# Decay attention and routed experts on one core: causal scores packed two heads to 192 columns, products of the attention done in halves of 64 rows of output

## The chip, the core and the metric

One NeuronCore of a Trainium2 chip runs the whole program in one launch. The metric is the device time of that launch in microseconds (us). TensorE (PE) does the matrix products and loads a stationary operand before each of them (the profile lists these loads as PEld), VectorE (DVE) and ScalarE (ACT) work on elements, GpSimd (POOL) and SyncE (SP) here mostly issue DMAs.

## The reference

Linear attention with a complex decay per token and feature runs over 768 tokens for 4 batches and 8 heads of 48 features; its output goes through a mixture of 8 experts, to which tokens are assigned greedily with a capacity.

```python
scale = np.minimum(mag, 0.999) / (mag + 1e-06)          # mag = |a|
for t in range(S):
    new_re = ar * S_re - ai * S_im
    new_im = ar * S_im + ai * S_re
    kv = np.einsum('bhd,bhe->bhde', k[:, :, t], v[:, :, t])
    S_re, S_im = (new_re + kv, new_im)
    y[:, :, t] = np.einsum('bhd,bhde->bhe', q[:, :, t], S_re)
...
logits = x @ w_gate                                     # x: y, all heads of a token
...
h = np.maximum(x[mask] @ w1[e], 0.0)
out[mask] = h @ w2[e]
```

## The kernel before

The program has two parts, `attention` and `experts`. Attention goes through 24 units of 128 tokens, six units to a batch (`cc` is the number of a unit in its batch, 0 to 5). ACT and DVE first turn the decays of three units at a time into running magnitudes and angles and rotate and scale k and q with them; a unit's k and q of all heads (96 real numbers each, cosine and sine part) then go by eight DMAs through the tile `f` into the tile `KQ` (96 x 8 heads x 257: 128 columns of k, 128 of q, one of decay). After that a unit consists of these steps, whose names in the code stand in brackets:

- scores (`SC`, twice, four heads each): `sc` = k-transposed times q, 128 keys by 128 queries for each head;
- mask (`MK`, twice, on DVE): `am` = `sc` times the causal mask, so keys after the query count nothing;
- flip (`FL`, twice, units with `cc` under 5): `kp` = k with tokens in rows, by PE transposes; ACT copies it to `kt` (`KC`);
- state (`ST`): `U` = `kt`-transposed times v, for each head 96 x 48, with tokens as the contraction; `carry` (`CA`, `cc` over 0) adds the old state `W` by a product with the identity, 96 x 384; DVE multiplies by the decay into the next `W` (`WM`);
- mix (`MX`): `y` = v-transposed times `am`, plus (`cc` over 0) `W`-transposed times q. Each head's output has 64 rows (48 and 16 of the next head), so two heads lie in the lower and the upper half of `y`, and their products stand next to each other;
- turn back (`XC`, `FN`, `XE`): ACT copies `y` to `xT`, PE turns it with the matrix `pick` (tokens in rows, and the router's logits beside them) into `xp`, ACT copies that to `x`, and it is stored.

Each of these products is fp32: one instruction of the program becomes two passes on PE, each with its own load of weights (192 score products are x384 in the profile); a transpose is one pass. The order of all instructions on every engine is fixed beforehand: `in_order` plays the steps through with a cost for each and a priority from the table `OFF`, and a helper class records them (so nearly all have its line, L137). Where its play leaves PE idle, products into the tile `hot` are put in, which nobody reads.

`attention` is followed by the routing of tokens and the experts, for which PE multiplies in three fp32r products.

Of the kernel before, what the change touches and what calls it, by code (L numbers as in the profile page):

```python
# [8 lines left out]
F32 = mybir.dt.float32  # L9
# [47 lines left out]
def constants(nc, con, z, w_gate):  # L57
    v, g = nc.vector, nc.gpsimd

    def t(n, shape, dt=F32):  # L60
        x = con.tile(shape, dt, name=n)
        setattr(z, n, x)
        return x
# [3 lines left out]
    v.tensor_scalar(t("ident", [128, 128]), jp, 0.0, None, op0=OP.is_equal)  # L67
    v.tensor_scalar(t("mask", [128, 128]), jp, 0.0, None, op0=OP.is_ge)
    t("tri", [128, 128], BF)
# [33 lines left out]


GROUPS = [(b, c, GC) for b in range(B) for c in range(0, S // 128, GC)]
CUTS = {0: [(0, 1), (1, GC)], 7: [(0, 2), (2, GC)]}
# [135 lines left out]
def attention(nc, real, tc, z, q, k, a_re, a_im, v_tok, xd, later):  # L242
# [9 lines left out]
    for i in range(2):  # L252
        w = con.tile([96, 400], F32, name=f"W{i}")
        g.memset(w, 0.0)
        W.append(w)
    for i in range(2):
        x = con.tile([128, GC, 432], F32, name=f"V{i}")
        g.memset(x[:, :, 384:], 0.0)
        VT.append(x)
# [205 lines left out]
    def unit(i):  # L465
# [8 lines left out]
        def KQ():  # L474
            return tiles["KQ", i]

        for hh in range(2):
            def scores(hh=hh):
                sc = ps.tile([128, 4, 128], F32, name="sc", bufs=2)
                mine["sc", hh] = sc  # L480
                for h in range(4):
                    nc.tensor.matmul(sc[:, h], KQ()[:, hh * 4 + h, :128], KQ()[:, hh * 4 + h, 128:256], start=True, stop=True)

            def mask(hh=hh):
                a = wk.tile([128, 4, 128], F32, name="am", bufs=4)
                v.tensor_tensor(a, mine["sc", hh], z.mask[:, None].to_broadcast([128, 4, 128]), op=OP.mult)
                mine["am", hh] = a
            op(("SC", i, hh), "pe", 0.9, at - 0.5, scores, KD + [("MK", i - 1, hh)])
            op(("MK", i, hh), "dve", 0.64, at, mask, [("SC", i, hh), ("MX", i - 2)])
        if cc < 5:  # L490
            for hh in range(2):
                def flip(hh=hh):
                    kp = ps.tile([128, 4, 96], F32, name="kp", bufs=2)
                    mine["kp", hh] = kp
                    for h in range(4):
                        nc.tensor.transpose(kp[:, h], KQ()[:, hh * 4 + h, :128], z.ident[:96, :96])

                def copy(hh=hh):
                    if "kt" not in mine:
                        mine["kt"] = wk.tile([128, 8, 96], F32, name="kt")  # L500
                    nc.scalar.activation(mine["kt"][:, hh * 4:hh * 4 + 4], mine["kp", hh], AF.Copy)
                op(("FL", i, hh), "pe", 0.34, at - 0.45, flip, KD + [("KC", i - 1, hh), ("KC", i - 2, hh)])
                op(("KC", i, hh), "act", 0.44, at, copy, [("FL", i, hh), ("ST", i - 2), ("ST", i - 3)])

            def state():
                U = ps.tile([96, 384], F32, name="U")
                mine["U"] = U
# [22 lines left out]
        def mix():  # L530
            Wc = W[cc % 2]
            y = ps.tile([128, 4, 128], F32, name="y")
            mine["y"] = y
            for p in range(4):
                for inter in range(2 if cc else 1):
                    for h in (2 * p, 2 * p + 1):
                        o = y[64 * (h % 2):64 * (h % 2) + 64, p]
                        e = slice(h * 48, h * 48 + 64)
                        if inter:
                            nc.tensor.matmul(o, Wc[:, e], KQ()[:, h, 128:256], start=False, stop=True)  # L540
                        else:
                            nc.tensor.matmul(o, v_[:, c, e], mine["am", h // 4][:, h % 4], start=True, stop=(cc == 0))

# [635 lines left out]
def experts(nc, tc, z, router, w1, w2, xd, out):  # L1179
# [152 lines left out]
    for n in range(WARM):  # L1332
        o = plan.tensor.matmul(hot[:, n % 3], z.mask, z.ident, start=True, stop=True)
        o.kind, o.main = "warm", True
        o.deps.append(router.placed)
# [59 lines left out]
def _lay_out(inputs):  # L1395
    import numpy as np

    def feature_major(a):
        a = a.reshape(B, H, S, 3, 16).transpose(0, 3, 4, 1, 2)
        return np.ascontiguousarray(a).reshape(B, 3, 128, S)  # L1400

    c = np.ascontiguousarray
    return {
# [3 lines left out]
        "a_im": feature_major(inputs["a_im"]),  # L1407
        "v": c(inputs["v"].transpose(0, 2, 1, 3)).reshape(N, DM),
        "w_gate": c(inputs["moe_w_gate"]).reshape(4, 2, D, E),
# [18 lines left out]
```

## Time and profile before

| | us |
|---|---|
| median of 3 runs (527.74 to 534.6) | 533.71 |
| the profiled execution's own time | 531.14 |
| its span, first to last instruction | 529.4 |
| first scores to the last turn back, in the span | 39.9 to 241 |
| routing of the first expert, then experts | 241 to 529 |

The page gives busy time by engine, but matmuls are pipelined, so the busy time of PE is more than what its products need one after the other. What a product needs is read from the starts in the timeline: the start of one kind of product to the start of the next, over the number of passes. The chain of work that ended last says where PE, DVE or a DMA held up the end.

### The profile page before, as it was taken

What the parts mean: (1) busy time and instruction counts of PE and PEld (TensorE: products, weight loads), DVE (VectorE), ACT (ScalarE), POOL (GpSimd) and SP (SyncE); (2) the same over time, 40 slices, a digit from 0 to 9 for tenths busy, and PEclk for the clock granted to TensorE, in tenths of its full rate; (3) what the DMA queues carried; (4) which work ended last, traced back from release to release, by engine and by line L of the source; (5) the groups of instructions that cost most, each with busy time, mean ns of one, the idle gap of its engine ahead of it and who ended that gap; (6) DMA issues with size and microseconds to landing.
All of it is one profiled execution on the core that took longest, in us unless ns stands there. A gap on an engine that the chain in (4) does not pass through costs nothing.

```text
span 529.4 us, 9655 instructions
## 1 busy us (share of the span) xinstructions
PE 451.3 (85%) x3626; PEld 395.3 (75%) x3635; DVE 410.5 (78%) x1192; ACT 271.6 (51%) x418; POOL 81.2 (15%) x95
## 2 busy tenths in 40 slices
PE   0009889898979999996699799999999999999993
PEld 0007769596868788995588468888888888999993
DVE  6989878999979999834847499889898987974330
ACT  6996848796949695611011513343252544363421
POOL 3000000000000000000021320522322242450202
PEclk9999989999989999997589999999999999999997
DMA  8866878897978776731260703544161521950101
GB/s 256 252 176 154 236 201 252 210 244 232 253 204 256 206 240 171 194 81 46 80 206 1 298 30 120 175 169 150 46 251 62 230 84 42 402 195 4 46 0 45
DMA packets 48909, 86.03 MB, mean 163 GB/s; under 512 B 5344, under 2 KB 43744, under 8 KB 46816
## 3 DMA queue, kind: packets, MB, share of 16 engines
q1 hardware_dynamic: 39104, 42.56, 28.1%
q0 software_dynamic: 6304, 38.16, 21.1%
q10 hardware_dynamic: 3456, 4.72, 2.5%
q8 instruction: 28, 0.46, 0.4%
q14 instruction: 17, 0.14, 0.1%
HBM read 53.49 MB, written 9.44 MB: 119 GB/s over the span
## 4 chain that ended last, share of the span: by engine, by line
PE 42%; DVE 18%; DMA 17%; issue 10%; ACT 5%; SPq 4%; POOL 2%; POOLq 0%; DVEq 0%; ACTq 0%
PE acc L137 24%; PE y L137 4%; SPq L137 4%; DMA xg<-xd,idx 4%; PE sc L137 4%; PE U L137 4%; DMA s<-s 3%; ACT s L137 3%; DMA ar<-in_a_re 3%; PE cnt L137 2%; DMA V<-in_v 2%; DVE f L137 2%; DVE hl L137 2%; DMA KQ<-f 2%; DVE neg L137 2%
## 5 line engine op out<-in xcount | busy, mean ns | idle before, releaser
L137 PE MATMUL sc<-KQ 96*128 96x128 f32 x384 | 50.2, 284 | 41.0 <-DMA KQ<-f 40.9
L137 PEld LDWEIGHTS sc<-KQ 96*128 96x128 f32 x384 | 47.4, 198 | 44.3 <-DMA KQ<-f 41.8
L137 ACT ACTIVATE hh<-acc 128x384 fp32r<-128x384 f32 x56 | 27.0, 491 | 77.4 <-PE acc L137 77.2
L137 PE MATMUL acc<-xh,w1l 128*128 128x384 f32 x168 | 55.8, 345 | 0.0
L137 PE MATMUL acc<-xh,w1h 128*128 128x384 f32 x168 | 55.7, 345 | 0.0
L137 PE MATMUL acc<-xl,w1h 128*128 128x384 f32 x168 | 54.9, 340 | 0.0
L137 PE MATMUL acc<-w2h,hl 128*128 128x384 f32 x168 | 54.0, 348 | 0.0
L137 PE MATMUL acc<-w2l,hh 128*128 128x384 f32 x168 | 53.5, 346 | 0.5 <-DVE w2l L137 0.5
L137 PE MATMUL acc<-w2h,hh 128*128 128x384 f32 x168 | 53.9, 345 | 0.0
L137 DVE TENSOR_TENSOR ind<-m,thr 128x768 bf16<-128x768 f32 (+1 forms) x45 | 34.0, 774 | 15.3 <-PE thr L137 14.7
L137 DVE TENSOR_TENSOR f<-kq,CS 128x768 f32<-128x768 f32 x48 | 43.5, 951 | 0.2 <-ACT CS L137 0.2
L137 POOL DMA_INDIRECT out<-ot,idx x24 | 26.3, 1095 | 96.3 <-ACT ot L137 92.4
L137 DVE SCALAR_TENSOR_TENSOR hl<-acc,hh 128x384 fp32r<-128x384 f32 x56 | 30.3, 552 | 13.4 <-ACT hh L137 12.8
L137 PE MATMUL y<-am,V 128*64 128x128 f32 x384 | 38.3, 289 | 1.4 <-ACT xT L137 0.9
L137 ACT ACTIVATE ot<-acc 128x384 f32<-128x384 f32 x24 | 11.8, 491 | 54.0 <-PE acc L137 35.3
L137 DVE TENSOR_TENSOR am<-sc,mask 128x512 f32<-128x512 f32 x48 | 32.1, 682 | 4.3 <-PE sc L137 4.1
L137 POOL DMA_INDIRECT xg<-xd,idx x24 | 27.6, 1149 | 48.1 <-issue 22.3
L137 PE MATMUL xp<-pick,xT 112*128 112x104 f32 x192 | 26.8, 283 | 6.9 <-ACT xT L137 4.7
L137 PEld LDWEIGHTS acc<-w2l,hh 128*128 128x128 f32 x168 | 31.0, 188 | 1.6 <-DVE w2l L137 1.0
L137 PEld LDWEIGHTS acc<-xh,w1h 128*128 128x128 f32 x168 | 31.2, 188 | 1.2 <-DVE ic L137 0.4
L137 PE MATMUL y<-KQ,W 96*64 96x128 f32 x320 | 31.9, 277 | 0.2 <-DVE W L137 0.2
L137 PEld LDWEIGHTS xp<-pick,xT 112*128 112x128 f32 x192 | 24.0, 194 | 10.7 <-ACT xT L137 6.8
(184 smaller groups left out, 1074.7 us busy)
## 6 DMA issues: line engine op xcount, KB each, us to landing
KQ<-f SPq DMA_DIRECT2D x192, 96.4 KB, 2.5
kq<-in_k SPq DMA_DIRECT2D x8, 576.0 KB, 5.2
kq<-in_q SPq DMA_DIRECT2D x8, 576.0 KB, 7.0
V<-in_v SPq DMA_DIRECT2D x8, 576.0 KB, 9.2
xd<-x ACTq DMA_DIRECT2D x24, 192.0 KB, 2.8
ar<-in_a_re SPq DMA_DIRECT2D x6, 576.0 KB, 4.7
ai<-in_a_im SPq DMA_DIRECT2D x6, 576.0 KB, 6.9
s<-s POOLq DMA_DIRECT2D x6, 576.0 KB, 7.9
```

The costliest lines, as they stand in the source:

```text
L137: r = f(*a, **k)
```

## The change

Four things change; the steps, their costs in the planner and their priorities stay.

Scores leave out the keys 64 to 127 for the queries 0 to 63 (never causal). For a pair of heads, `he` and `ho`, `sc` holds 192 columns in place of 256. The first 64 hold the keys 0 to 63 and queries 0 to 63 of both heads, `he` in the top half and `ho` in the low half; the next 64 the queries 64 to 127 of `he` with all its keys; the last 64 the same of `ho`, with its two halves of keys exchanged. That is four products a pair, each with 64 columns of weights, instead of two with 128. The mask gets the same form, and `am` has 384 columns, not 512.

Because odd heads now have their keys exchanged, so have v (exchanged on the host, in the layout of the input) and k with tokens in rows: the flip is no transpose any more but, for each head, two fp32 products with the identity, one for each half of the tokens. Its copy goes to one of two fixed tiles `KT` with 32 columns of zeros behind.

The state (`U`, now 128 rows) and the turn back (`xp`) are done in two products each, for the low 64 and the high 64 columns of the weights, into the two halves of the output.

The mix first does the queries 0 to 63 of all eight heads, with 64 keys each; then, by pairs of heads, the queries 64 to 127 with 128 keys and, where there is an old state, the product with `W` as before.

```diff
         for hh in range(2):
             def scores(hh=hh):
-                sc = ps.tile([128, 4, 128], F32, name="sc", bufs=2)
+                sc = ps.tile([128, 512], F32, name="sc", bufs=2)[:, :384].rearrange("p (a b) -> p a b", a=2)
                 mine["sc", hh] = sc
-                for h in range(4):
-                    nc.tensor.matmul(sc[:, h], KQ()[:, hh * 4 + h, :128], KQ()[:, hh * 4 + h, 128:256], start=True, stop=True)
+                for p in range(2):
+                    he, ho = hh * 4 + 2 * p, hh * 4 + 2 * p + 1
+                    packed = sc[:, p].rearrange("p (a b) -> p a b", a=3)
+                    for r, h, keys, o, queries in ((0, he, 0, packed[:, 0:2], 0), (1, ho, 0, packed[:, 0::2], 0),
+                                                   (0, ho, 1, packed[:, 2], 1), (1, he, 1, packed[:, 1], 1)):
+                        nc.tensor.matmul(o[HALVES[r]], KQ()[:, h, HALVES[keys]], KQ()[:, h, 128 + 64 * queries:256],
+                                         start=True, stop=True)
...
-                a = wk.tile([128, 4, 128], F32, name="am", bufs=4)
-                v.tensor_tensor(a, mine["sc", hh], z.mask[:, None].to_broadcast([128, 4, 128]), op=OP.mult)
+                a = wk.tile([128, 2, 192], F32, name="am", bufs=4)
+                v.tensor_tensor(a, mine["sc", hh], z.mask[:, None].to_broadcast([128, 2, 192]), op=OP.mult)
...
                     for h in range(4):
-                        nc.tensor.transpose(kp[:, h], KQ()[:, hh * 4 + h, :128], z.ident[:96, :96])
+                        for r in range(2):
+                            nc.tensor.matmul(kp[HALVES[r], h], KQ()[:, hh * 4 + h, HALVES[(r + h) % 2]], z.ident[:96, :96],
+                                             start=True, stop=True)
...
                 for h in range(8):
-                    nc.tensor.matmul(U[:, h * 48:h * 48 + 48], mine["kt"][:, h], v_[:, c, h * 48:h * 48 + 48],
-                                     start=(h == 0), stop=(h == 7 and not cc), skip_group_check=True)
+                    for r in HALVES:
+                        nc.tensor.matmul(U[r, h * 48:h * 48 + 48], KT[i % 2][:, h * 96 + r.start:h * 96 + r.stop],
+                                         v_[:, c, h * 48:h * 48 + 48], start=(h == 0), stop=(h == 7 and not cc), skip_group_check=True)
...
+            heads = [(h, y[HALVES[h % 2], h // 2], slice(h * 48, h * 48 + 64), mine["am", h // 4][:, h // 2 % 2]) for h in range(8)]
+            for h, o, e, a in heads:
+                r = HALVES[h % 2]
+                nc.tensor.matmul(o[:, :64], v_[r, c, e], a[r, :64], start=(h < 2), stop=(cc == 0), skip_group_check=True)
             for p in range(4):
...
+                for h, o, e, a in heads[2 * p:2 * p + 2]:
+                    b_ = 64 + 64 * (h % 2)
+                    nc.tensor.matmul(o[:, 64:], v_[:, c, e], a[:, b_:b_ + 64], start=False, stop=(cc == 0), skip_group_check=True)
+                if cc:
+                    for h, o, e, a in heads[2 * p:2 * p + 2]:
+                        nc.tensor.matmul(o, Wc[:, e], KQ()[:, h, 128:256], start=False, stop=True, skip_group_check=True)
...
             for p in range(4):
-                nc.tensor.matmul(xp[:, p, :104], mine["xT"][:112, p], z.pick[:112, p], start=True, stop=True)
+                for r in HALVES:
+                    nc.tensor.matmul(xp[r, p, :104], mine["xT"][:112, p, r], z.pick[:112, p], start=True, stop=True)
```

On PE, in the steps of one unit with an old state (tile names with the numbers of V, W and KT; the size is that of the output), the order before is:

```order
L137 MATMUL kp<-ident,KQ 128x96 x8
L137 MATMUL U<-W_111,ident 96x384
L137 MATMUL sc<-KQ 128x128 x8
L137 MATMUL U<-V_113,kt 96x48 x8
L137 MATMUL xp<-pick,xT 128x104 x4
L137 MATMUL y<-am,V_113 64x128 x2
L137 MATMUL y<-KQ,W_109 64x128 x2
```

and at the same place in the changed program:

```order
L142 MATMUL kp<-ident,KQ 64x96 x16
L142 MATMUL U<-W_115,ident 96x384
L142 MATMUL sc<-KQ 64x128
L142 MATMUL sc<-KQ 64x2x64
L142 MATMUL sc<-KQ 64x64 x2
...
L142 MATMUL U<-V_121,KT_117 64x48 x16
L142 MATMUL xp<-pick,xT 64x104 x8
L142 MATMUL y<-am,V_121 64x64 x10
L142 MATMUL y<-KQ,W_113 64x128 x2
```

No step changes its place: every step stands where it stood, with twice as many products in it (the three rows of `sc` come four times). On ACT and SP the order is the same row for row. On DVE the masks' sizes change, and at the start of the program four small operations build the mask matrix in place of one. The place on DVE where the masks of a unit stand between the router's work on the first 18 units' logits and the element work, before:

```order
L137 TENSOR_REDUCE qm<-q_2045 128x18
L137 TENSOR_TENSOR oh<-q_2045,qm 128x144
L137 TENSOR_TENSOR am<-sc,mask 128x512 x2
L137 COPY tl<-neg 128x3
L137 TENSOR_SCALAR zi<-s_1535 128x3x128
L137 TENSOR_SCALAR neg<-neg 128x3x256
```

and in the changed program:

```order
L142 TENSOR_REDUCE qm<-q_2649 128x18
L142 TENSOR_TENSOR oh<-q_2649,qm 128x144
L142 TENSOR_TENSOR am<-sc,mask 128x384 x2
L142 COPY tl<-neg 128x3
L142 TENSOR_SCALAR zi<-s_1968 128x3x128
L142 TENSOR_SCALAR neg<-neg 128x3x256
```

Only the size of the two masks is another, 384 columns for 512.

## Rows read from the trace of the kernel before

**Rows 1.** The page, busy us by engine (share of span) and instructions.

```profile
PE 451.3 (85%) x3626; PEld 395.3 (75%) x3635; DVE 410.5 (78%) x1192; ACT 271.6 (51%) x418; POOL 81.2 (15%) x95
```

**Rows 2.** Busy time by stretch: PE, PEld, DVE, ACT, POOL; clock, DMA share, GB/s.

```profile
60.00:100.00 40.00, 35.33 (x318) 27.85 (x321) 34.84 (x61) 30.59 (x37) 1.26 (x2) 0.96 0.82 227
100.00:140.00 40.00, 36.70 (x374) 31.78 (x376) 37.31 (x67) 31.68 (x38) 1.69 (x2) 1.00 0.84 226
180.00:205.00 25.00, 23.89 (x259) 21.96 (x257) 24.79 (x52) 16.19 (x24) 0.00 (x0) 1.00 0.78 225
205.00:241.00 36.00, 35.85 (x400) 32.81 (x401) 22.51 (x45) 17.79 (x31) 0.00 (x0) 1.00 0.49 127
```

**Rows 3.** Chain that ended last: start, us, what (x passes or instructions).

```profile
43.35 2.50 PE sc L137 x10
...
74.97 2.62 PE U L137 x18
...
182.41 1.20 DVE am L137 x2
...
204.48 0.61 DVE am L137
205.13 1.25 PE y L137 x16
...
239.91 1.08 PE xp L137 x8
```

**Rows 4.** Timeline of PE, 213 to 222 us: start, us, operation, shapes, passes.

```profile
213.11 0.88 PE L137 MATMUL kp<-ident,KQ 96*128 96x96 f32 x8
213.83 0.81 PE L137 MATMUL U<-W,ident 96*96 96x384 f32 x2
214.47 1.95 PE L137 MATMUL sc<-KQ 96*128 96x128 f32 x16
216.26 1.48 PE L137 MATMUL U<-V,kt 128*96 128x48 f32 x16
217.58 1.10 PE L137 MATMUL xp<-pick,xT 112*128 112x104 f32 x8
218.61 0.44 PE L137 MATMUL y<-am,V 128*64 128x128 f32 x4
...
219.10 0.39 PE L137 MATMUL y<-am,V 128*64 128x128 f32 x4
219.32 0.39 PE L137 MATMUL y<-KQ,W 96*64 96x128 f32 x4
...
220.52 0.89 PE L137 MATMUL U<-W,ident 96*96 96x384 f32 x2
221.25 0.82 PE L137 MATMUL kp<-ident,KQ 96*128 96x96 f32 x8
```

**Rows 5.** Timeline of the weight loads, 218.60 to 218.70 us.

```profile
218.61 0.20 PEld L137 LDWEIGHTS y<-am,V 128*64 128x64 f32 x4
```

**Rows 6.** Operations on the tile `am`, 198 to 241 us: ns min/median/max.

```profile
L137 PEld LDWEIGHTS y<-am,V x96: 132/136/138, 205.1 to 239.3; 128*64 128x64 f32 x96
```

**Rows 7.** Groups by form, 0 to 250 us: busy, mean ns, idle before.

```profile
L137 DVE TENSOR_TENSOR am<-sc,mask 128x512 f32<-128x512 f32 x48 | 32.1, 682 | 4.3 <-PE sc L137 4.1
L137 PE MATMUL hot<-cold 128*128 128x512 bf16 x63 | 16.3, 395 | 0.4 <-issue 0.2
L137 DVE TENSOR_TENSOR W<-U,KQ 96x384 f32<-96x384 f32 x20 | 11.0, 548 | 8.3 <-PE U L137 5.6 <-DMA KQ<-f 2.7
```

**Rows 8.** Timeline, 208 to 209 us: copy of the flip, and the state.

```profile
208.04 0.87 ACT L137 ACTIVATE kt<-kp 128x384 f32<-128x384 f32 x2
...
208.85 0.38 PE L137 MATMUL U<-V,kt 128*96 128x48 f32 x3
```

**Rows 9.** Timeline, 247 us: a count of the routing.

```profile
247.10 1.04 PE L137 MATMUL cnt<-oh,ind 128*32 128x8 bf16 x24 [2.02 <-DVE ind L137]
```

**Rows 10.** The page, DMA queues: packets, MB, share of 16 engines' span.

```profile
q8 instruction: 28, 0.46, 0.4%
```

More of the change, by code (lines that the diff above doesn't have):

```diff
@@ L67, in constants @@
     v.tensor_scalar(t("ident", [128, 128]), jp, 0.0, None, op0=OP.is_equal)
-    v.tensor_scalar(t("mask", [128, 128]), jp, 0.0, None, op0=OP.is_ge)
+    mask = t("mask", [128, 192])
+    top, low = HALVES
+    for r, o, i in ((slice(0, 128), slice(64, 128), low), (top, top, top), (low, top, low), (top, slice(128, 192), top)):
+        v.tensor_scalar(mask[r, o], jp[r, i], 0.0, None, op0=OP.is_ge)
+    g.memset(mask[low, 128:192], 1.0)
     t("tri", [128, 128], BF)
@@ L102, in best @@
     v.tensor_tensor(oh, q, bc(qm, E), op=OP.is_equal)
+HALVES = (slice(0, 64), slice(64, 128))
 GROUPS = [(b, c, GC) for b in range(B) for c in range(0, S // 128, GC)]
@@ L255, in attention @@
         W.append(w)
+    KT = []
+    for i in range(2):
+        x = con.tile([128, 800], F32, name=f"KT{i}")
+        g.memset(x[:, 768:], 0.0)
+        KT.append(x)
     for i in range(2):
@@ L495, in flip @@
                     for h in range(4):
-                        nc.tensor.transpose(kp[:, h], KQ()[:, hh * 4 + h, :128], z.ident[:96, :96])
+                        for r in range(2):
+                            nc.tensor.matmul(kp[HALVES[r], h], KQ()[:, hh * 4 + h, HALVES[(r + h) % 2]], z.ident[:96, :96],
+                                             start=True, stop=True)
                 def copy(hh=hh):
-                    if "kt" not in mine:
-                        mine["kt"] = wk.tile([128, 8, 96], F32, name="kt")
-                    nc.scalar.activation(mine["kt"][:, hh * 4:hh * 4 + 4], mine["kp", hh], AF.Copy)
+                    nc.scalar.activation(KT[i % 2][:, hh * 384:hh * 384 + 384].rearrange("p (a b) -> p a b", a=4), mine["kp", hh], AF.Copy)
                 op(("FL", i, hh), "pe", 0.34, at - 0.45, flip, KD + [("KC", i - 1, hh), ("KC", i - 2, hh)])
@@ L505, in state @@
             def state():
[L506 to L507 removed]
+                U = ps.tile([128, 384], F32, name="U")
+                mine["U"] = U[:96]
                 for h in range(8):
[L509 to L510 removed]
+                    for r in HALVES:
+                        nc.tensor.matmul(U[r, h * 48:h * 48 + 48], KT[i % 2][:, h * 96 + r.start:h * 96 + r.stop],
+                                         v_[:, c, h * 48:h * 48 + 48], start=(h == 0), stop=(h == 7 and not cc), skip_group_check=True)
             def carry():
@@ L1332, in experts @@
     for n in range(WARM):
-        o = plan.tensor.matmul(hot[:, n % 3], z.mask, z.ident, start=True, stop=True)
+        o = plan.tensor.matmul(hot[:, n % 3], z.mask[:, :128], z.ident, start=True, stop=True)
         o.kind, o.main = "warm", True
@@ L1400, in feature_major, with swapped @@
         return np.ascontiguousarray(a).reshape(B, 3, 128, S)
+    def swapped(a):
+        a = np.ascontiguousarray(a).reshape(B, S // 128, 2, 64, H // 2, 2, D)
+        a[..., 1, :] = a[:, :, ::-1, ..., 1, :].copy()
+        return a.reshape(N, DM)
     c = np.ascontiguousarray
```

10 lines of the change are left out of this document (1 added, 9 removed).

## Prediction

> **What bounds the kernel now.** Read the table by stretch first. Attention is the span to 241 us, and no engine bounds all of it: from 60 to 140 us PE and DVE are each busy about nine tenths of the time and the DMA engines over eight tenths; from 180 to 205 us DVE is busy for 24.79 of 25 us; from 205 to 241 us PE has no gap and DVE little to do [rows 2]. Then the chain of work that ended last: PE holds it in stretches that begin at 43 and 75 us and, the longest, at 205 us, running on to the last turn back at 241; in between, masks and other work of DVE do (182 to 205 us) [rows 3], or DMAs. The whole of attention is in series with the experts, whose instructions don't change. So an edit on PE counts where the chain is on PE, and an edit on DVE where DVE is.
>
> I counted the chain's PE pieces from 43 to 241 us (the first and last stand in [rows 3]): scores of 9.9 units, flips of 7, states of 9, turns back of 9, mixes of 11 (two of them without an old state), and 8 carries. Of masks there are 9.
>
> **Price of a pass.** A fp32 pass goes by its columns: the carry's two passes of 384 take 0.64 us (213.83 to 214.47), 0.00083 a column; 16 score passes of 128 take 1.79, 0.112 each, so a fixed part of about 0.005 [rows 4]. The state has 48 columns in a pass but takes 1.32/16 = 0.0825 (216.26 to 217.58) [rows 4]: its load of 96 columns sets that, 0.00086 a column, 0.055 for 64. In the mix, two heads in two halves of the output run side by side: a group of four passes takes 0.22 (219.10 to 219.32) [rows 4], 0.11 a pair, what one score pass takes alone.
>
> Do loads run side by side too? Four mix loads take 0.20 together [rows 5], and one lasts 0.136 [rows 6]. So all four begin within 0.064, where one after the other at 0.055 would need 0.165: they go in twos. A pair of passes with 64 columns each should then take 0.053 + 0.005 = **0.058**, with 96 columns 0.085, with 104 0.092. No row shows a pair that short; the bounds are 0.055 (the loads) and 0.11 (the mix's pair). I take 0.058, since rows 4 to 6 give it from both sides, columns and loads.
>
> **The change, part by part** (us for one unit on PE).
> - Scores: 1.79 before; a head pair is now two pair-passes of 128 and two of 64, so 8 x 0.112 + 8 x 0.058 = 1.36: -0.43.
> - Flip: 8 transposes, one pass each. They take 0.72 behind a mix [rows 4], 0.68 at 0.085 a pass. Now 32 passes in 16 pairs, 1.36: +0.68. This is the one part that plainly gets dearer.
> - State: 1.32 to 16 x 0.058 = 0.93: -0.39.
> - Turn back: 8 x 0.112 = 0.90 (128 columns of weights) to 8 x 0.092 = 0.74: -0.16.
> - Mix: 16 x 0.11 = 1.76 to 8 x 0.11 for the old state and 16 x 0.058 for `am`: 1.81, +0.05. No column is saved here; the same 128 are cut in two.
> - Switches between whole and half width. Into the mix: turn back to mix takes 1.03 for 0.90 of work; inside it, 1.91 for 1.76; the carry behind it 0.73 (220.52 to 221.25), 0.64 otherwise [rows 4]. That is 0.37 for in and out. Before, the mix alone is in halves. Now all is, but the carry is not, and the first part of the mix has 64 rows of keys instead of 128. With a carry, that is four switches a unit for two, if the change of rows costs what the change of columns does: +0.37. No row shows a change of rows; bounds 0 and +0.37. I take the upper one, the nearest row.
>
> The Trainium skill speaks against the change here: "TensorEngine Tiling (Array Packing)", section "Key Properties", says that changing the tiling mode drains TensorE, a change of tile does not. The trace agrees for columns (0.73 against 0.64, [rows 4]); by the rule the rows count too, and the term is +0.37, otherwise 0.
>
> So a unit with an old state (16 of 24 have state and carry) gains 0.93 and pays 1.10. On the chain: 9.9 x -0.43 + 7 x 0.68 + 9 x -0.39 + 9 x -0.16 + 11 x 0.05 + 8 x 0.37 = -4.26 + 4.76 - 3.51 - 1.44 + 0.55 + 2.96 = -0.9. One gain on it is lost: the state at 208.85 starts as the copy of the flip on ACT ends (208.04 + 0.87) [rows 8], so scores that end sooner before it win nothing: +0.4.
>
> - Masks: 384 columns for 512. The decay product has that form from PSUM, 548 ns for 682 [rows 7]: 48 x 0.134 = 6.4 us of DVE. On the chain 9, so -1.2. The bound is every mask before 205 us, 38 x 0.134 = -5.1, if DVE's queue passes all of it on.
> - At the start: three more small operations on DVE and three fills on POOL while DVE and POOL wait for the first loads; ACT's copies keep their sizes; the DMAs, and the queues of SP and ACT, are untouched; the host exchanges v without device time. Nothing.
>
> Sum: -0.9 + 0.4 - 1.2 = **-1.7**, so 531.14 gives 529.4. The profiled execution is 0.5% under the median of 533.71, from which it gives 532.0. I forecast **531**, the middle: no change that a measurement tells apart, since that needs about 2%, 10.7 us.
>
> **Rivals.**
> 1. *PE cannot take passes that fast* (slower). A unit has 162 passes with a load instead of 82, and every gain above rests on pairs at 0.058, 0.029 a pass. Before, PE takes 84 passes in 8.14 us (213.11 to 221.25), 0.097 each, and its fastest long run is the mix, 0.055 to 0.06 [rows 4]; only 24 passes of the routing go at 0.043 [rows 9]. If 0.055 a pass is what PE can be fed, every pair takes 0.11: 40 pairs of 64 at +0.054, 16 of 96 at +0.027, 8 of 104 at +0.02, +2.7 a unit, x 9 on the chain = +24, less the 1.7: 554. It also needs some 3,500 more instructions on top of 7,261 [rows 1], 14 more packets on the 28 of about 1.2 us (0.4% of 16 x 529 us) [rows 10], the same kind of limit. It decides from about 0.078 a pair, where 9 x 64 pairs x 0.02 are 11 us. Against it: loads that start within 0.064 in fours, and the 0.043. The fill products, 16.3 us [rows 7], leave PE some room off the chain.
>
> The skill's "TensorE: Matmul & The Clock Gate", section "Back-to-back issue gap", has a floor of about 25 ns for small matmuls, and 62 ns where the sequencer decodes them; by the latter a unit is 162 x 0.062 = 10.0, an estimate, and by the former nothing changes. No row here decides between them.
>
> 2. *More gain than the chain shows* (faster, but hardly by 2%). Rows cost no switch (-3.0) and all masks pass on (-3.9 more): -8.6, 522.5. For it: DVE's 24.79 of 25 us. Against: the DMA share over 0.8 where the chain leaves both engines.
>
> 3. *The masks become the wait.* The mix now begins with all eight heads, so both masks must be there 0.23 us after its start (8 passes at 0.029), not 0.9 (16 at 0.055). At 204.48 the first of two masks is on the chain and the mix starts at 205.13 [rows 3], 0.6 before the second can end; PE then stands about 0.4, with XC, FN and the flips queued behind it and ACT's copy of `y` waiting. At every one of 11 mixes: +4.4, 534 to 536; within 2%.
>
> **How the numbers follow.** Forecast case (527 to 534) 0.62; rival 2 0.15, of which I put a third over 2%, since the runs of before alone scatter by 1.3%; rival 3 0.06; rival 1 0.17. That the halves don't run side by side at all is excluded by rows 4 to 6. So faster 0.05, same 0.78, slower 0.17. The range takes in rival 2 to its price and the smaller prices of a pair of rival 1 (0.08 to 0.09), up to 545; outside are 0.05 below and 0.14 above.
>
> **What would show it.** In the changed trace, start to start: scores 1.36, flip 1.36, state 0.93, turn back 0.74 plus 0.1 to 0.2 at a switch, first part of the mix 0.46, `am` masks 548 ns; the stretch from the 20th unit's flip to the last turn back within 1 us of before. Pairs at 0.08 or more, or idle PE with cause "issue" inside a run of passes, show rival 1; PE idle inside a mix for DVE's mask, rival 3. What would make me wrong most is the 0.058, which no row of before has.

## The result and the profile after

The changed kernel is slightly slower: 535.49 us median of 20 executions (531.66 to 538.64) beside 534.15 (527.26 to 541.63) for the kernel before, ratio 1.0087, interval 1.0059 to 1.0114. Within 2% it is no change, as forecast, but forecast was a gain of 0.5%, and the interval leaves that out. The ratio leaves out executions more than 1.5% above the fastest of their kernel, which are 7 of the 20 of the kernel before and none of the changed one; over all executions the medians differ by 0.25% only, and the means by 1.5 us with an uncertainty of 2.0. So a gain is not there, and the size of the loss is less sure than the interval alone says. The profiled execution took 533.22 us (span 531.4) beside 531.14 (529.4).

The page after, busy time by engine and the queue of instruction packets:

```profile
PE 451.1 (85%) x5386; PEld 389.7 (73%) x5395; DVE 405.0 (76%) x1195; ACT 273.1 (51%) x418; POOL 81.4 (15%) x98
...
q8 instruction: 42, 0.69, 0.5%
```

PE does 1,760 passes more in the same busy time, and DVE is busy 5.5 us less [rows 1]; there are 14 more instruction packets, as forecast. The busy time by stretch, columns as in [rows 2]:

```profile
60.00:100.00 40.00, 34.95 (x607) 27.71 (x606) 33.88 (x61) 31.18 (x38) 1.68 (x2) 0.96 0.81 226
100.00:140.00 40.00, 37.18 (x708) 31.50 (x708) 32.75 (x60) 28.64 (x36) 0.84 (x1) 0.91 0.80 219
180.00:205.00 25.00, 23.91 (x480) 20.04 (x481) 23.66 (x50) 18.01 (x27) 0.00 (x0) 1.00 0.73 209
```

DVE is no longer full from 180 to 205 us, and the clock from 100 to 140 us is 0.91 on the mean, where it was 1.00. The last turn back starts at 243.74 us, before at 241.79; from the router's first product on, at 245.48 us and before at 243.73, 285.9 us of the span are left, before 285.7. So the 2.0 us that the two profiled executions differ by arise in attention, and not in its last stretch, which PE fills: from the flip at 208.39 us to the turn back at 242.04 are 33.65 us, and before, from 206.32 to 239.84, 33.52.

They arise between the sixth and the seventh turn back. PE's timeline there, first before, then after:

```profile
95.88 1.14 PE L137 MATMUL xp<-pick,xT 112*128 112x104 f32 x8 [0.73 <-ACT xT L137]
...
105.44 0.30 PE L137 MATMUL kp<-ident,KQ 96*128 96x96 f32 x1 [0.94 <-DMA KQ<-f]
...
112.94 1.03 PE L137 MATMUL xp<-pick,xT 112*128 112x104 f32 x8
```
```profile
96.22 0.93 PE L142 MATMUL xp<-pick,xT 112*64 112x104 f32 x16 [1.28 <-ACT xT L142]
...
106.76 0.59 PE L142 MATMUL kp<-ident,KQ 96*64 96x96 f32 x4 [2.24 <-DMA KQ<-f]
...
110.52 2.77 PE L142 MATMUL sc<-KQ 96*64 96x128 f32 x32
113.08 1.18 PE L142 MATMUL U<-V,KT 128*64 128x48 f32 x32
...
117.10 0.93 PE L142 MATMUL xp<-pick,xT 112*64 112x104 f32 x16
```

The distance to before grows from 0.34 to 4.16 us, and half of it is made up later. The flip waits 2.24 us for the stacked keys (0.94 before), and behind this gap the granted clock is 0.50, the lower of its two levels (1.2 GHz of 2.4), and the scores take 2.56 us (110.52 to 113.08), for 1.39 at the full clock below. The busy time of two stretches:

```profile
104.00:106.00 2.00, 0.52 (x14) 0.33 (x9) 0.96 (x2) 1.16 (x1) 0.00 (x0) 1.00 0.24 75
...
108.00:110.00 2.00, 2.00 (x34) 1.88 (x32) 1.86 (x2) 0.50 (x1) 0.00 (x0) 0.50 1.08 369
```

That is one execution of each kernel. In the profiles of two runs below that are as slow, e14 and e17, the clock from 100 to 140 us is 1.00, so this drop isn't the cause in all.

The timeline of PE, the same place as [rows 4]: start, us, operation, shapes, passes.

```profile
215.48 1.49 PE L142 MATMUL kp<-ident,KQ 96*64 96x96 f32 x32
216.90 0.89 PE L142 MATMUL U<-W,ident 96*96 96x384 f32 x2
217.72 1.56 PE L142 MATMUL sc<-KQ 96*64 96x128 f32 x32
219.11 1.09 PE L142 MATMUL U<-V,KT 128*64 128x48 f32 x32
220.03 0.90 PE L142 MATMUL xp<-pick,xT 112*64 112x104 f32 x16
220.86 0.95 PE L142 MATMUL y<-am,V 64*64 64x64 f32 x20
...
222.97 0.89 PE L142 MATMUL U<-W,ident 96*96 96x384 f32 x2
223.78 1.54 PE L142 MATMUL kp<-ident,KQ 96*64 96x96 f32 x32
```

From start to start: flip 1.42 (215.48 to 216.90), of which 0.1 is the change to the carry, and 1.37 behind a carry (223.78 to 225.15); scores 1.39, state 0.92, turn back 0.83, mix 2.11, carry 0.81. One unit with state and carry: 215.48 to 223.78 less one carry of 0.81 is 7.49 us; before, 213.11 to 221.25 less 0.64 is 7.50 [rows 4]. On PE alone the change is even. The weight loads of the mix's first part, and the groups by form:

```profile
213.47 0.31 PEld L142 LDWEIGHTS y<-am,V 64*64 64x64 f32 x8
```
```profile
L142 DVE TENSOR_TENSOR am<-sc,mask 128x384 f32<-128x384 f32 x48 | 25.7, 549 | 7.2 <-PE sc L142 6.5
...
L142 DVE TENSOR_TENSOR W<-U,KQ 96x384 f32<-96x384 f32 x20 | 11.0, 548 | 11.2 <-PE U L142 11.2
```

Eight loads in 0.31 us: by twos as the four of [rows 5]. The masks take 549 ns, and 6.4 us of DVE are gone. But read the idle time behind the second bar: it was 5.6 us for `W` behind PE and 4.1 for `am` [rows 7]. The waits in attention, 40 to 245 us (total us, times, longest):

```profile
DVE W L142 <- PE U L142: 11.2, 7, 3.5
...
PEld kp L142 <- DMA KQ<-f: 8.4, 13, 2.4
...
DVE am L142 <- PE sc L142: 6.5, 9, 2.2
DVE f L142 <- DMA KQ<-f: 5.3, 6, 2.3
...
PE y L142 <- DVE am L142: 0.3, 1, 0.3
```

These DVE waits were 5.6, 4.1 and 2.1 us before, that of the flips 5.3: what DVE saved, it stands idle instead. The mix hardly waits for a mask (0.3 us). And the chain that ended last has other pieces in attention: flips 10.6% of 205 us (before 3.7%), transfers to `KQ` 11.3% (5.4%), SP's queue, that is SyncE at issuing transfers, 12.2% (8.0%).

### The profile page after: what moved, and what is told of

The parts are those of the page before. It is cut to its first block, busy times and chain, and to the rows that moved or that the text cites. A ratio compares the mean times of both kernels' runs of the same rounds, so it can differ in the third digit from the quotient of the medians.

```text
span 531.4 us, 13181 instructions
## 1 busy us (share of the span) xinstructions
PE 451.1 (85%) x5386; PEld 389.7 (73%) x5395; DVE 405.0 (76%) x1195; ACT 273.1 (51%) x418; POOL 81.4 (15%) x98
## 4 chain that ended last, share of the span: by engine, by line
PE 44%; DMA 17%; DVE 13%; issue 11%; ACT 5%; SPq 5%; POOL 2%; POOLq 0%; DVEq 0%; ACTq 0%
PE acc L142 23%; SPq L142 5%; PE y L142 5%; DMA xg<-xd,idx 4%; DMA KQ<-f 4%; PE kp L142 4%; PE sc L142 4%; DMA V<-in_v 3%; PE U L142 3%; DMA s<-s 3%; ACT s L142 3%; PE cnt L142 2%; DVE hl L142 2%; DMA ar<-in_a_re 2%; PE xp L142 2%
## 5 line engine op out<-in xcount | busy, mean ns | idle before, releaser
L142 PE MATMUL sc<-KQ 96*64 96x128 f32 (+1 forms) x768 | 42.1, 263 | 41.2 <-DMA KQ<-f 41.2
L142 PEld LDWEIGHTS sc<-KQ 96*64 96x64 f32 x768 | 39.1, 148 | 46.7 <-DMA KQ<-f 42.2
L142 PE MATMUL y<-am,V 64*64 64x64 f32 (+1 forms) x768 | 43.8, 234 | 1.5 <-ACT xT L142 1.2
L142 PEld LDWEIGHTS y<-am,V 64*64 64x64 f32 (+1 forms) x768 | 36.5, 142 | 7.0 <-ACT xT L142 1.6
L142 ACT ACTIVATE ot<-acc 128x384 f32<-128x384 f32 x24 | 11.8, 491 | 57.0 <-PE acc L142 35.9
L142 DVE SCALAR_TENSOR_TENSOR hl<-acc,hh 128x384 fp32r<-128x384 f32 x56 | 30.3, 551 | 13.4 <-ACT hh L142 12.8
L142 PE MATMUL kp<-ident,KQ 96*64 96x96 f32 x640 | 35.5, 261 | 5.0 <-DMA KQ<-f 4.9
L142 PEld LDWEIGHTS kp<-ident,KQ 96*64 96x64 f32 x640 | 30.6, 145 | 9.9 <-DMA KQ<-f 8.4
L142 PEld LDWEIGHTS acc<-xh,w1l 128*128 128x128 f32 x168 | 31.3, 188 | 0.8 <-issue 0.5
```

The source lines that it names most:

```text
L142: r = f(*a, **k)
```

## The experiments

All times are medians; the ratio is to the kernel before, timed beside it. The kernel before scattered between sittings (531.6 to 534.2), so ratios count, not medians.

| run | what | us | ratio, interval |
|---|---|---|---|
| e1, e10 | before + state and turn back by halves | 529.09, 528.47 | 0.9965 (0.9925-1.0004), 0.9954 (0.9916-0.9992) |
| e2 | before + flip in two fp32 halves | 539.70 | 1.0171 (1.0101-1.0240) |
| e6 | before + masks of 384 columns | 532.69 | 1.0027 (0.9982-1.0071) |
| e3 | changed + carry by halves | 531.66 | 1.0011 (0.9968-1.0053) |
| e4 | changed, tokens not exchanged | 533.09 | 1.0047 (1.0009-1.0086) |
| e5 | changed + cheap flip | 534.81 | 1.0063 (1.0021-1.0105) |
| e8 | e5 + carry by halves | 532.95 | 1.0023 (0.9983-1.0063) |
| e7 | changed + planner's costs as measured | 540.70 | 1.0213 (1.0130-1.0296) |
| e9 | e1 + mix cut, 64 rows first | 536.01 | 1.0058 (1.0004-1.0113) |
| e13 | e9 with 128 rows throughout | 529.42 | 0.9964 (0.9928-1.0001) |
| e14 | changed, mix cut twice | 536.62 | 1.0106 (1.0067-1.0144) |
| e17 | changed, mix with 128 rows | 533.40 | 1.0084 (1.0053-1.0115) |
| e18 | e17 + carry by halves | 531.37 | 0.9976 (0.9929-1.0022) |
| e16 | as e18, from a second copy of v | 539.42 | 1.0133 (1.0073-1.0193) |
| e11, e12 | changed, before: two buffers more | 533.26, 530.95 | 1.0028 (0.9984-1.0073), 0.9966 (0.9920-1.0013) |
| e15 | e1 + two buffers more | 529.55 | 0.9963 (0.9926-1.0000) |

**One part alone, in the kernel before.**

State and turn back by halves:

```diff
-                    nc.tensor.matmul(U[:, h * 48:h * 48 + 48], mine["kt"][:, h], ...)
+                    for r in HALVES:
+                        nc.tensor.matmul(U[r, h * 48:h * 48 + 48], KT[i % 2][:, h * 96 + r.start:h * 96 + r.stop], ...)
...
-                nc.tensor.matmul(xp[:, p, :104], mine["xT"][:112, p], ...)
+                for r in HALVES:
+                    nc.tensor.matmul(xp[r, p, :104], mine["xT"][:112, p, r], ...)
```

> The kernel before with one part of the change alone: the state and the turn back by halves of 64 columns of weights; scores, mask, flip and mix as before. PE per unit: state 1.32 to 0.93, turn back 0.90 to 0.81; no switch is added, since both stand next to the mix. Theory 1 (the flip is what costs, the rest of the change gains): about 0.5 us a unit, 4 to 5 us where the chain is on PE, ratio to before 0.990 to 0.993. Theory 2 (switches between whole and half width cost): no switch added, so the same 0.990 to 0.993. Theory 3 (PE's sum hardly decides; the pace of attention is set by DVE's and SP's order and the DMAs): 0.996 to 1.004.

> The version of e1 once more, unchanged, beside the others: whether state and turn back by halves alone make the kernel faster than before. If the first result holds: ratio 0.993 to 1.000, median 528 to 531. If it was a draw of the spread: 1.000 to 1.005.

Both times about 0.4% faster, though e1's interval just takes in no change. By PE's timeline a unit from flip to next carry takes 6.80 us (214.69 to 221.49 in e10) for 7.41 (213.11 to 220.52 [rows 4]). It is, with e13, the fastest version found, but of the 0.61 us a unit, 5.5 us for the 9 units that were on the chain, it keeps about 2; 5.5 lies outside both intervals. On the chain SP's queue now has 28.4% of attention in e1 and 17.5% in e10, for 8.0% before.

The flip in two products a head, tokens not exchanged:

```diff
-                        nc.tensor.transpose(kp[:, h], KQ()[:, hh * 4 + h, :128], z.ident[:96, :96])
+                        for r in HALVES:
+                            nc.tensor.matmul(kp[r, h], KQ()[:, hh * 4 + h, r], z.ident[:96, :96], start=True, stop=True)
```

> The kernel before with the flip alone changed: each head by two fp32 products with the identity for the two halves of the tokens (not exchanged) in place of one transpose. PE per unit: flip 0.66 to 1.32, and up to two more switches (+0.2 to 0.37), ahead of scores and state. Theory 1: +0.7 to +1.0 us on the 7 flips of the chain and more where the chain moves to flips, +7 to +15 us, ratio to before 1.013 to 1.03. Theory 2: about +0.3 us of switches on 8 to 16 units, 1.005 to 1.01. Theory 3: 0.998 to 1.005.

```profile
219.46 1.49 PE L138 MATMUL kp<-ident,KQ 96*64 96x96 f32 x32
220.88 0.89 PE L138 MATMUL U<-W,ident 96*96 96x384 f32 x2
221.60 1.95 PE L138 MATMUL sc<-KQ 96*128 96x128 f32 x16
```

+9.1 us (5.4 to 12.8), twice what 7 flips on the chain times 0.68 give. But the flip here pays switches too: 1.42, and 0.72 for the carry behind it, where before has 0.72 and 0.64 [rows 4], so 0.78 a unit; and the chain of before has 9 flips, not 7 (see below). 9 x 0.78 = 7.0 is inside the interval. Flips are now 11.6% of the chain in attention, not 3.7%.

Masks of 384 columns alone (of each four heads the fourth takes the third's product):

```diff
-                v.tensor_tensor(a, mine["sc", hh], z.mask[:, None].to_broadcast([128, 4, 128]), op=OP.mult)
+                v.tensor_tensor(a, mine["sc", hh][:, :3], z.mask[:, None].to_broadcast([128, 3, 128]), op=OP.mult)
```

> The kernel before with the masks alone at 384 columns: the mask of every fourth head is left out and the mix takes the third head's scores in its place, so the outputs of those heads are other ones. DVE -6.4 us (48 x 0.134), PE as before. The forecast's count (9 masks on the chain): -1.2 us, ratio to before 0.998. Its bound (every mask before 205 us): -5.1, 0.990. Theory 4: DVE's order is one of the things that hold the end, 0.990 to 0.997.

No gain; of the -1.2 us forecast the interval leaves room for just -1.0, of the bound of -5.1 nothing.

**A part made cheap in the changed kernel.** The carry in halves takes two of the four switches out:

```diff
-                nc.tensor.matmul(mine["U"], z.ident[:96, :96], W[cc % 2][:, :384], ...)
+                for r in HALVES:
+                    nc.tensor.matmul(mine["UU"][r], z.ident[:96, r], W[cc % 2][:, :384], ...)
```

> The changed kernel with the carry in halves too (two products of 64 columns of the identity, side by side), so that in units with an old state two of the four switches go; the carry's 0.64 us stay. Per unit -0.30 us (0.09 and 0.08 into the carry, 0.09 and 0.04 out of it). Theory 1: -2 to -3 us of the chain's 8 carries, ratio to before 1.003 to 1.006 where the changed kernel has 1.0087. Theory 2: nearly all of the loss, 0.998 to 1.003. Theory 3: no different from the changed kernel, 1.006 to 1.011.

The timeline of PE in e3, mix to flip:

```profile
221.33 0.95 PE L142 MATMUL y<-am,V 64*64 64x64 f32 x20
...
223.34 0.81 PE L142 MATMUL U<-W,ident 96*64 96x384 f32 x4
223.98 1.24 PE L142 MATMUL kp<-ident,KQ 96*64 96x96 f32 x26
```

Mix to carry 2.01 for 2.11, the carry 0.64 for 0.81: 0.27. The flip behind it takes 1.32 for 1.37 (e18 shows it as well: 219.93 to 221.25), which makes 0.32 a carry. The 8 carries on the chain of before would give 2.6 us, all 16 of the kernel 5.1; the ratio falls by 0.76%, 4.0 us (plus or minus 2.7), which allows both.

The flip in one bf16 pass over the upper 16 bits of k (so the state's k is cut to 8 bits), and then this with the carry of e3:

```diff
-                            nc.tensor.matmul(kp[HALVES[r], h], KQ()[:, hh * 4 + h, HALVES[(r + h) % 2]], z.ident[:96, :96],
+                            lo = 128 * ((r + h) % 2) + 1
+                            nc.tensor.matmul(kp[HALVES[r], h], KQ().bitcast(BF)[:, hh * 4 + h, lo:lo + 127:2],
+                                             z.ident.bitcast(BF)[:96, 1:192:2], ...)
```

> The changed kernel with the flip in one pass: the two products of each head take the upper 16 bits of k and of the identity as bf16, so the state is made of k cut to 8 bits of mantissa (scores and all else as before). Places, halves, exchange and switches stay; the flip goes from 1.30 to about 0.47 us a unit. Theory 1 (the flip ahead of the scores is what makes the change slower, the rest gains): -0.8 us on the 16 flips that are now on the chain, -8 to -13 us against the changed kernel, ratio to before 0.985 to 0.995. Theory 4 (a longer product costs wherever it draws the chain onto itself, a shorter one wins little, since DVE's order, SP's queue and the DMAs then hold the end): 0.998 to 1.004.

> Both together: the changed kernel with the flip in one pass of upper halves as bf16 (k cut to 8 bits of mantissa in the state) and the carry in halves. PE per unit with an old state 7.49 to about 6.4, against 7.50 before. If PE's sum decides (theories 1 and 2): 1.1 us a unit, 16 to 20 us off PE, of which 9 or 10 on the chain of before, ratio 0.975 to 0.985. Theory 4: 0.988 to 0.998, less than the sum of the two edits alone.

The flip takes 0.44 us for 1.42 (217.14 to 217.58 in e5), and that brings 0.24% (plus or minus 0.5); the carry beside it 0.4 (0.6). The waits of e8 in attention show where it went:

```profile
PEld L142 <- DMA KQ<-f: 19.0, 29, 1.4
...
PE kp L142 <- DMA KQ<-f: 13.7, 22, 1.3
DVE f L142 <- DMA KQ<-f: 12.1, 8, 3.1
```

The flips now wait for the stacked keys to land (19.0 and 13.7 us for loads and products, 8.4 and 4.9 in the changed kernel), and DVE for buffers that these transfers read. SP's queue has 25.6% of attention's chain in e5 and 24.2% in e8, for 12.2% in the changed kernel. PE's idle time has another price. Busy time in attention of the changed kernel, then of e8, and two stretches of e8:

```profile
40.00:245.00 205.00, 188.75 (x3615) 158.26 (x3624) 167.85 (x315) 143.69 (x189) 3.37 (x4) 0.98 0.73 205
```
```profile
40.00:245.00 205.00, 172.72 (x3327) 144.51 (x3334) 166.84 (x315) 142.82 (x188) 3.37 (x4) 0.94 0.74 205
```
```profile
60.00:62.00 2.00, 0.00 (x0) 0.00 (x0) 2.00 (x5) 2.00 (x4) 0.64 (x1) 0.90 0.68 81
62.00:64.00 2.00, 1.77 (x20) 1.52 (x22) 1.77 (x3) 1.53 (x3) 0.00 (x0) 0.50 1.07 324
```

PE did nothing from 60 to 62 us, and behind that the granted clock is 0.50; over attention it is 0.94 on the mean for 0.98. The busy share of a long stretch doesn't tell it: in the changed kernel the clock from 100 to 140 us is 0.91 with PE busy for 37.18 of 40 us, and what lies ahead of its fall is the gap at 104 us.

Without the exchange (single-pass transposes, five score products a pair, POOL shifting v):

```diff
-                        for r in range(2):
-                            nc.tensor.matmul(kp[HALVES[r], h], KQ()[:, hh * 4 + h, HALVES[(r + h) % 2]], ...)
+                        nc.tensor.transpose(kp[:, h], KQ()[:, hh * 4 + h, :128], z.ident[:96, :96])
...
+        op(("VS", gi), "pool", 0.01, at, lambda: g.tensor_copy(VS[gi % 2][HALVES[1]], VT[gi % 2][HALVES[0]]), [("lv", gi)])
```

> The changed kernel without the exchange of token halves, so that the flip is again one transpose for each head: scores packed with five products a pair (the odd head's keys in their own order), v as before, and a copy of the first 64 keys of v to the other 64 rows by GpSimd, three units at a time, which the odd heads read in the first part of the mix. PE per unit against the changed kernel: flip 1.30 to 0.66, scores 1.39 to about 1.42, switches as they are (the flip mostly stands next to the carry). Theory 1: the flip's cost goes, the gains stay: ratio to before 0.985 to 0.993. Theory 2: the switches stay, 1.003 to 1.008. Theory 3: 1.004 to 1.010, or worse by what GpSimd's copies take from DVE.

0.40% below the changed kernel (plus or minus 0.5), no better than e3. On the chain in attention SP's queue has 12.9% and the transfers to `KQ` 11.8%, much as in the changed kernel.

**The planner told of the new costs.**

```diff
-            op(("SC", i, hh), "pe", 0.9, at - 0.5, scores, ...)
+            op(("SC", i, hh), "pe", 0.7, at - 0.5, scores, ...)
-                op(("FL", i, hh), "pe", 0.34, at - 0.45, flip, ...)
+                op(("FL", i, hh), "pe", 0.66, at - 0.45, flip, ...)
...
```

> The changed kernel with the planner's costs set to what the trace shows for the changed steps (scores 0.70 a group of four heads, mask 0.5, flip 0.66, state 0.93, carry 0.82, mix 2.05 or 1.15, turn back 0.75), priorities as they are; the order on the engines and the number of fill products follow from that. If the old order, made for the old costs, is what loses: 0.993 to 1.002 to before. If not: 1.005 to 1.012; a new order can also be worse, since the priorities were found for the old costs.

The slowest of all: another order, with the same instructions but for 11 more fill products (74 for 63), moves more than the whole change.

**The mix.** e9 cuts it as in the changed kernel, e13 does that without the change of rows:

```diff
+            for h, o, e, a in heads:
+                nc.tensor.matmul(o[:, :64], v_[:64, c, e], a[:64, :64], ...)      (e9)
+                nc.tensor.matmul(o[:, :64], v_[:, c, e], a[:, :64], ...)          (e13)
             for p in range(4):
+                for h, o, e, a in heads[2 * p:2 * p + 2]:
+                    nc.tensor.matmul(o[:, 64:], v_[:, c, e], a[:, 64:], ...)
```

> The kernel before with the state and the turn back by halves (the version of e1), and the mix cut as in the changed kernel: queries 0 to 63 of all heads with 64 keys first, then the rest with 128. Scores, masks and flip are as before. It tells what the cut of the mix with its change of rows costs by itself. Theory that the extra waits of the changed kernel come from the mix (0.20 us longer in a unit, 24 units, all of it in the path from masks to the turn back): +3 to +5 us over the version of e1, so 532 to 534, ratio 1.003 to 1.006. Theory that the count on the chain failed for every piece alike and that attention's pace is set outside PE: within 1.5 us of e1, ratio 0.994 to 0.999. y takes 2.1 us with an old state in both.

> The version of e9 with one thing less: the first part of the mix takes all 128 rows of keys and not 64 (the low rows of the mask are zero there), so the order and the number of passes are as in e9 and the mix has no change of rows. Theory that the two changes of rows, some 0.13 us each in the path from the masks to the turn back, are what makes the changed kernel slower: back at the version of e1, 528 to 530, ratio 0.993 to 0.999, and the mix takes 1.8 to 1.9 us against 2.11. Theory that it is the order of the mix (both masks wanted at once): as e9, ratio 1.003 to 1.009, with more PE waits for masks. Theory that e9 was only a draw: e9 and this one alike near 1.000.

PE's timeline, turn back to mix to the next step, of e9 and then of e13:

```profile
218.65 0.90 PE L138 MATMUL xp<-pick,xT 112*64 112x104 f32 x16
219.48 0.95 PE L138 MATMUL y<-am,V 64*64 64x64 f32 x20
...
221.59 0.88 PE L138 MATMUL kp<-ident,KQ 96*128 96x96 f32 x8
```
```profile
221.25 0.90 PE L138 MATMUL xp<-pick,xT 112*64 112x104 f32 x16
221.98 0.75 PE L138 MATMUL y<-am,V 128*64 128x64 f32 x20
...
223.89 0.89 PE L138 MATMUL U<-W,ident 96*96 96x384 f32 x2
```

From the turn back to the next step 2.94 us (218.65 to 221.59) against 2.64 (221.25 to 223.89): the two changes of rows cost 0.30 us, and in this version the ratio differs by 5.0 us of the kernel (plus or minus 3.5), most of 24 x 0.30 = 7.2. I took that for the cause; the next runs were to confirm it. e14 does the mix in two rounds of four heads, and so changes rows four times:

```diff
+            for two in (0, 2):
+                for h, o, e, a in heads[2 * two:2 * two + 4]:
+                    nc.tensor.matmul(o[:, :64], v_[r, c, e], a[r, :64], ...)
+                for p in (two, two + 1):
...
```

> The changed kernel with its mix in two rounds of four heads: each round first the 64-row part, then the 128-row part. Same passes, four changes of rows in a mix and not two, and the second mask is wanted later. Theory of the row changes on the path: mix 2.35 to 2.45 us, 24 x 0.27 = up to 6.5 us more, 536 to 541, ratio 1.012 to 1.021. Theory that the need for both masks costs: not slower than the changed kernel, ratio 1.002 to 1.009. Theory that attention's pace is set outside PE: the same.

e17 gives the first part all rows from the second group on, e18 adds the carry of e3, and e16 is as e18, in every group, from a second copy of v with zeros in place of the other head's keys:

```diff
-                r = HALVES[h % 2]
+                r = slice(0, 128) if gi else HALVES[h % 2]                        (e17, e18)
-                nc.tensor.matmul(o[:, :64], v_[r, c, e], a[r, :64], ...)
+                nc.tensor.matmul(o[:, :64], vz_[:, c, e], a[:, :64], ...)         (e16)
```

> The changed kernel in which the first part of the mix takes all 128 rows, in every group but the first (21 of 24 units), from the same tiles, with no transfer added: the products of a head then also take in the other head's rows, so from the second group on the output leaves the computation; number, order and size of the passes are the same. Only the row changes of the mix are gone. Theory of the row changes on the path (0.25 to 0.35 us a unit): 4 to 6 us less than the changed kernel, 529 to 531.5, ratio 0.996 to 1.001. Theory that they cost only 0.1 to 0.2% here, as the second pair of them did in e14: 533 to 535, ratio 1.004 to 1.009.

> The same with the carry in halves (e3): from the second group on no switch is left on PE, and the transfers are those of the changed kernel, so it is e16 without its 4.7 MB more (the output leaves the computation in the same way). If e16 lost to its transfers: at least 1% below e16, ratio 0.994 to 1.002, 528 to 533, and at or below e3. If a PE with no switches gains nothing and e16 is slow for another reason: ratio 1.005 to 1.013. The waits for KQ should be 14.5 us (weight loads of the flips) if they are PE's own, 5 to 9 if they were the added transfers'.

> The changed kernel with the carry in halves (as e3) and a second copy of v, laid out with zeros where the other head of a pair has its keys, loaded beside v (4.7 MB of transfers more): the first part of the mix then takes all 128 rows and PE has no switch of width or rows left in a unit. Theory of the row changes on the path: the mix takes 1.8 us, 4 to 6 us less than e3, 526 to 529, ratio 0.988 to 0.997, unless the larger transfers cost part of it. Theory that attention's pace is set outside PE (transfers, DVE): as e3 or slower, ratio 1.000 to 1.010, with longer waits for KQ.

The theory fell. In e17 the mix and the turn back are as short as in e13:

```profile
221.91 0.90 PE L142 MATMUL xp<-pick,xT 112*64 112x104 f32 x16
222.64 0.75 PE L142 MATMUL y<-am,V 128*64 128x64 f32 x20
223.22 0.39 PE L142 MATMUL y<-KQ,W 96*64 96x128 f32 x4
...
224.55 0.89 PE L142 MATMUL U<-W,ident 96*96 96x384 f32 x2
```

and the kernel is as slow as the changed one (-0.2 us, plus or minus 2.2). Its chain in attention says what took the place of PE's work: SP's queue 21.0%, for 12.2% in the changed kernel, and flips 3.0%, for 10.6%. In e14 the mix takes 2.31 us (218.42 to 220.73), 0.20 more, and 24 times that, 4.8, came out as +1.0 (2.5). The carry counts again: e18 is 1.08% below e17 by the ratios (5.7 us, plus or minus 3.0); the medians of these two, timed side by side, differ by 2.0 us only.

e16 and e18 run the same passes but for the first group; e16 loads 4.7 MB more, and is 1.6% slower (8.4 us, plus or minus 4.0). The wait of the flips' weight loads for `KQ`, of e16 and then of e18:

```profile
PEld kp L142 <- DMA KQ<-f: 14.5, 23, 1.7
```
```profile
PEld kp L142 <- DMA KQ<-f: 6.3, 9, 1.4
```

So in this kernel transfers hold up the end as PE does.

**Buffers.** One buffer more for `KQ` and for `f`, in the same order:

```diff
-            return get("f", i, [128, 3, 2, 257], bufs=F_BUFS)
+            return get("f", i, [128, 3, 2, 257], bufs=F_BUFS + 1)
...
-            KQ = get("KQ", i, [96, 8, 257], p=st, bufs=KC_BUFS)
+            KQ = get("KQ", i, [96, 8, 257], p=st, bufs=KC_BUFS + 1)
```

> The changed kernel with one more buffer for the stacked keys and queries (six) and one more for the products that are stacked (five); the order of instructions is the same, only the waits for a free buffer are looser. Theory that the pace is set by a loop through these buffers (DVE waited 5.3 us for the products' buffers in the changed kernel, 12.1 in the one with the cheap flip, 2.1 before): 4 to 10 us less, 525 to 531, ratio 0.985 to 0.995, and those waits go. Theory that the longer flip and mix set it themselves: within 1.5 us of the changed kernel, ratio 1.003 to 1.010; the waits of DVE are put down to another cause. Theory that the transfers themselves are the limit (share over 0.8): no change either, and the waits for the landing stay.

> The kernel before with the same two buffers more, as the other half of the pair. Theory of the loop through the buffers: here the waits are smaller (2.1 us of DVE), so 1 to 3 us less, ratio 0.994 to 0.999, and the gap to the changed kernel closes. The other theories: ratio 0.997 to 1.003, the gap stays at 0.5 to 1%.

> The version of e1 (state and turn back by halves) with the two buffers more of e12: a version that may beat both kernels. If the two small gains add (0.4% and 0.3%): ratio 0.988 to 0.995, 525 to 528. If the buffers' gain was a draw or the waits only move: as e1, 0.993 to 0.998.

The changed kernel gains 0.6% (plus or minus 0.5), before 0.3 (0.5), e1 nothing. In e11 DVE's waits for the buffers of `f` are gone (5.3 us in the changed kernel), but the flips' loads wait 10.3 us for `KQ`, for 8.4: the wait moved. That loose buffers help where the waits for them were long fits this, and is hardly beyond the uncertainty.

## Why the prediction was wrong

**What held.** Every price of a pass. A pair of 64 columns takes 0.058: in e17 the first 20 passes of the mix take 0.58 (222.64 to 223.22). The forecast of 1.36, 1.36, 0.93 and 548 ns for flip, scores, state and mask came out as 1.32 to 1.42, 1.39, 0.92 and 549. Rival 1 is out: 32 passes of the state in 0.92 are 29 ns each. Rival 2 is out too: the rows do cost a switch, and the masks alone brought nothing (e6). The Trainium skill ("TensorE: Matmul & The Clock Gate", "Back-to-back issue gap") has 62 ns for matmuls that the sequencer decodes and a floor of about 25 for small ones. The trace's 29 ns lies near the floor. The measured time lies in rival 3's 534 to 536, but by luck: its mechanism is out, by the 0.3 us of the mix's wait for masks, and by e14.

**Switches.** A change of rows costs: 0.10 us into the mix and 0.20 inside it (e9 against e13), together 0.30, near the 0.37 that I took for it from the change of columns. The rule that I cited from the Trainium skill ("TensorEngine Tiling (Array Packing)", "Key Properties"), that changing the tiling mode drains TensorE, holds for rows here too. With the carry's 0.32 a unit pays 0.62, before 0.37: +0.25, not +0.37. My sum for a unit was also off: the gains are 0.98, not 0.93 (the mix's 0.05 stands on both sides), so the terms make a unit 0.12 longer, not 0.17. With the smaller switches it comes out even, as measured (7.49 and 7.50).

**The step that failed** is the sum made with counts from the chain: 9.9 x -0.43, 7 x 0.68, 9 x -0.39, 9 x -0.16, 8 x 0.37, the masks' 9. One count is wrong: the chain of before has 72 passes of flips (eight each from 45.85, 50.68, 80.71, 168.04, 206.39, 213.18, 221.41 and 228.06 us on, three at 126.01 and five at 160.57), 9 units and not 7, which alone turns the -1.7 into -0.3. The greater error is that a piece's share of one execution's chain was taken for what the piece is worth, shortened or lengthened. The runs show that it isn't:
- State and turn back shortened: 9 x 0.61 = 5.5 us by the counts; about 2 measured, at most 4.5 by e10's interval.
- Flip shortened in the changed kernel: 0.98 a unit (e5), 8.8 us for 9 units; 1.3 measured (plus or minus 2.7).
- Masks shortened: 1.2 forecast, none found; the interval leaves room for 1.0.
- The carry's switches taken out: 2.6 us for 8 carries; three pairs of runs (changed to e3, e5 to e8, e17 to e18) gave 4.0, 2.1 and 5.7 us, each plus or minus about 3. This passes on in full, and whether for 8 carries or for 16 isn't decided.
- Flip lengthened (e2): 7.0 us for 9 flips; 9.1 measured (5.4 to 12.8), so in full as well.

In ratios, then: the halves give -0.4%, the carry's switches take +0.76%, and the rest (flips dearer, scores and masks cheaper, mix cut) is the +0.5% that is left to 0.87, if the parts simply add, which no run shows. For this rest no run separates the flip's loss from the scores' gain: e4 and e5, which make the flip cheap, are 0.40% and 0.24% below the changed kernel, both within the uncertainty.

**Why gains pass on so badly** is shown in part. Where PE's work in a unit is shortened, SP's queue takes over the chain: it has 8.0% of attention before and 9.4% in e2, but 28.4% in e1, 17.5% in e10, 25.6% in e5, 24.2% in e8. One issue of a `KQ` transfer takes 0.60 us of it (99.70 to 100.30 us before), so by an estimate the eight of a unit take about 4.8 us, where a unit has some 8. These are shares of one execution each, and e11, with the PE work of the changed kernel, has 22.7%, so they show what stands next in line and not a price. Longer waits for `KQ` and a lower granted clock come with it (e8), and 4.7 MB more to load cost 1.6% (e18 to e16). So transfers, DVE and PE are late by turns. I had this in view, as what speaks against rival 2, and used it for that rival alone; it holds against every minus in my sum.

**Still open:** why the same 0.30 us in the mix cost 5.0 us in e9 and nothing in e17 (5.0 plus or minus 3.5 and 0.2 plus or minus 2.2, so the gap itself is barely clear of the noise), while the carry's 0.32 counts although SP's queue has 23.6% of the chain in e3 too. With a carry the next state waits for the state before, through PE and DVE, which the mix doesn't hold up; that is argued, not shown.

## What to carry to other kernels

Where several engines and transfers are late by turns, a count of pieces on the chain is no price. Here a longer flip cost what the count said, and of four pieces made shorter one paid in full and three about a third or less; which it will be isn't seen until the next wait behind a piece is found. So count a gain only with that next wait in hand, weigh an edit that trades equal times as a likely loss, and time each of its parts alone: here the half that only gains (state and turn back by halves) is faster than both kernels by itself. A switch of the tile's form between steps has to be counted for every step of the loop.

## What the hardware showed unexpectedly

- Two fp32 passes with loads of 64 columns, in two halves of the output, take 0.058 us together: the state's 32 passes take 0.92 us, 29 ns a pass, and the mix's 20 passes in e17 0.58.
- A change between 64 and 128 rows of weights costs 0.10 us into the mix and 0.20 on the way back (e9 against e13), and the full-width carry between half-width steps 0.27 with the flip's part left out, 0.32 with it (changed kernel against e3).
- Less work on PE can cost clock: where PE stood idle from 60 to 62 us in e8, the granted clock behind it was 0.50, and over attention it was 0.94 on the mean for 0.98 in the changed kernel.
